# Scores and maxima of two heads in 64-row tiles: a pooled attention with a second stage of matmuls

## The chip, the cores and the metric

The kernel runs on one core of a Trainium2 chip. A core has five engines that run side by side and wait for each other through semaphores: TensorE (PE in the profile; PEld is its weight load), VectorE (DVE), ScalarE (ACT), GpSimd (POOL) and SyncE (SP, which issues the DMAs here). TensorE writes to PSUM, eight banks of 512 fp32 values on each of 128 partitions; DVE and ACT read from there. The metric is the device time of one execution in microseconds.

## The reference

Eight batches, eight heads, 1152 positions, 64 values per head. Neighbouring queries are averaged first, so that 576 queries meet 1152 keys:

```
q_pool = q.reshape(B, H, S // 2, 2, D).mean(axis=3)
scores = matmul(q_pool, k.T) / sqrt(D)
scores = scores - max(scores, axis=-1)
attn   = exp(scores);  attn = attn / (sum(attn, axis=-1) + 1e-9)
x      = matmul(attn, v)          # then heads side by side: 4608 tokens x 512
h      = x @ w_in                 # 512 -> 2048
out    = (h - tanh(h)) @ w_out    # 2048 -> 512
```

All arrays are fp32, and the results are compared as such. The row maximum is needed exactly enough that the exponentials do not overflow or lose precision.

## The kernel before

**Two stages.** The first (attention) goes over 32 pairs of heads: a batch `b` and two neighbouring heads, whose 64 values each fill the 128 partitions. The second goes over ten chunks of up to 512 tokens with the hidden layer in 16 tiles of 128 (`hidden`, L522, and `second`, L547).

**hi and lo.** TensorE's quick format (fp32r) keeps fewer bits than fp32, so an operand is split into `hi` (rounded, by ACT) and `lo` (what is left, by DVE), and a product is the sum hi x hi + hi x lo + lo x hi.

**A pair's life before its scores.** `load` fetches q and k; `query_sums` (L203) adds neighbouring queries; `hi_part` and `lo_part` split 576 queries and 1152 keys. `max_queries` (L219) copies hi's queries by DMA into a block-diagonal array `bd` of 9 x 128 columns: the first head's 576 queries on partitions 0 to 63, the second's after them on 64 to 127. `operands` (L225) builds by ten DMAs the arrays `t1` (128 rows: lo and hi of keys above hi and lo of queries) and `t2` (66 rows: hi, and two rows that bring in the maximum). `max_part` (L241) multiplies `bd` tiles with hi's keys, 27 matmuls of 384 columns, two to a PSUM tile `ps_m`, and DVE reduces each tile to its maximum. `max_rows` (L251) combines them, splits them in hi and lo, turns them by a transpose, and sends them through `m_dram` to the last two rows of `t2`.

**A pair's scores.** `score_unit` (L281) makes 128 keys x 288 queries of one head in one bank `ps_s` by two matmuls (128 rows and 66 rows), and ACT takes the exponential. Six units (two heads, three key tiles) are a group; a pair has two halves of the queries with three groups each. `z_part` adds up a group's exponentials on POOL. `pv` (L302) multiplies them with v, two heads side by side in the columns of the array; v and the exponentials are plain fp32, so each such matmul leaves two records. `z_sums` sums over partitions, four column tiles side by side.

**Order.** All engines of the first stage follow an order that is written out by hand: `U = 36` units make a pair, and `add(u, f)` puts a piece of work at unit `u`; `first` holds what a unit does before its scores. The numbers in L438 to L469 place each pair's preparation ahead of it, some 100 units for the loads, 60 to 27 for the maxima. `w_block` (L371) also lies in these units: it prepares the two weight matrices in 32 blocks with a chain of DVE, POOL and ACT steps and stores them split to DRAM.

**PSUM.** Two tiles of two banks `ps_m`, three banks `ps_s`, one `ps_o`: eight.

**Into the second stage.** Near the end (L422 to L435) the first chunk's x and six tiles of weights are fetched; the weights go where the operands `t1` and `t2` of even pairs were. The other weights follow at L514 to L520. The second stage's own PSUM tiles take the same eight banks.

Of the kernel before, what the change touches and what calls it, by code (L numbers as in the profile page):

```python
# [43 lines left out]
def kernel(  # L44
# [51 lines left out]
    def load_x(tiles, sp, mul, hi, t0, n):  # L96
# [5 lines left out]
        def fetch(hp):  # L102
            x = xt.tile([P, 512], F32, name="x_f")
            r = xt.tile([P, 512], F32, name="x_r")
            t[hp] = x, r
# [20 lines left out]

    xp = [ctx.enter_context(tc.tile_pool(name="xp0", bufs=2))]
# [4 lines left out]
    op0 = ctx.enter_context(tc.tile_pool(name="op0", bufs=1))  # L132
# [8 lines left out]
    with ExitStack() as actx:  # L141

        wp = actx.enter_context(tc.tile_pool(name="wp", bufs=1))
# [20 lines left out]
        tt = [[o.tile([P, 2, KQ], F32R, name=f"t{j}_{i}") for j in (1, 2)] for i, o in enumerate((op0, op))]  # L164
        t1, t2 = [t[0] for t in tt], [t[1][0:66] for t in tt]


        bd = [op.tile([P, 9 * P], F32R, name=f"bd{i}") for i in range(2)]
        for i in range(2):
            nc.gpsimd.memset(bd[i].bitcast(F32), 0.0)  # L170
            nc.gpsimd.memset(t2[i][64:66, :, SQ:].bitcast(F32), 1.0)

        def raw_copy(dst, src):
            sp.dma_start(dst.bitcast(F32), src.bitcast(F32))


        at, first = {}, {}
# [10 lines left out]
        def load(pi):  # L188
# [3 lines left out]
            w.t2 = t2[w.i]  # L192
# [10 lines left out]
        def query_sums(pi, eng):  # L203

            w = pairs[pi]
            eng.tensor_tensor(w.kq[:, 0:SQ], w.q_n[:, 0], w.q_n[:, 1], op=ALU.add)
            w.mx = sm.tile([P, 9, 3], F32, name="mx")
            w.hi = x_tile(0)[:, 0:KQ]
            w.lo = ld.tile([P, KQ], F32R, name="kq_l")
# [15 lines left out]
        def operands(pi):  # L225

            w = pairs[pi]
            for h in range(2):
                r = slice(h * 64, h * 64 + 64)
                x1, x2 = t1[w.i][:, h], t2[w.i][:, h]  # L230
                raw_copy(x1[0:64, SQ:], w.lo[r, SQ:])
                raw_copy(x1[64:P, 0:SQ], w.lo[r, 0:SQ])
                raw_copy(x1[64:P, SQ:], w.hi[r, SQ:])
                raw_copy(x1[0:64, 0:SQ], w.hi[r, 0:SQ])
                raw_copy(x2[0:64], w.hi[r])

        spots = [((j, j + 5), (c,)) for c in range(3) for j in range(4)] + [((4,), (0, 1)), ((4,), (2,))]

        def max_part(u, pi, ts, cs):  # L241

            w = pairs[pi]
            ps = ps_m.tile([P, 2, 512], F32, name="ps_m")
            both = [(t, c) for t in ts for c in cs]
            for i, (t, c) in enumerate(both):
                pe.matmul(ps[:, i, 0:CH], bd[w.i][:, t * P:(t + 1) * P], w.hi[:, SQ + c * CH:SQ + (c + 1) * CH], start=True, stop=True)
            mx = w.mx[:, ts[0]:ts[-1] + 1:5, cs[0]] if len(ts) == 2 else w.mx[:, 4, cs[0]:cs[-1] + 1]
            add(u + 1, lambda: dve.tensor_reduce(mx, ps[:, 0:len(both), 0:CH], axis=AX.X, op=ALU.max), at=first)

        def max_rows(u, pi, steps):  # L251
# [11 lines left out]
            def turn():  # L263
                ps = w.ps_t = ps_m.tile([P, 2, 512], F32R, name="ps_m")[0:20, 0, 0:P]
# [8 lines left out]
            def back():  # L273

                sp.dma_start(w.t2[64:66, :, 0:SQ].bitcast(F32), md.rearrange("s (h n) -> s h n", h=2)[:, :, 0:SQ])
# [5 lines left out]
        def score_unit(w, half, h, kt, p):  # L281
# [3 lines left out]
            ps = ps_s.tile([P, 512], F32, name="ps_s")  # L285
            x1, x2 = t1[w.i][:, h], t2[w.i][:, h]
# [35 lines left out]
        def z_sums(u, w, hf):  # L322

            ps = ps_s.tile([P, 512], F32, name="ps_s")
# [13 lines left out]
        def z_out(u, w, hf, ps):  # L338

            act.activation(w.z_s[:, hf.n * HQ:(hf.n + 1) * HQ], ps[:, 0:HQ], AF.Copy)  # L340
            if hf.n == 1:
# [4 lines left out]
                if w.hp == NP - 1:  # L346
                    add(u + 6, lambda: tot.append((w.b, sums(w.b))))
                    if w.b < B - 1:
                        add(u + 22, lambda: reciprocals(dve, *tot[0]))
                        add(u + 25, lambda: spread(sp, *tot.pop(0)))  # L350
# [20 lines left out]
        def w_block(u, kind, r, c):  # L371
# [44 lines left out]
        for i, blk in enumerate(blocks):  # L416
            u = U // 2 + 34 * i
# [11 lines left out]
        spare = [t.rearrange("p h n -> p (h n)")[:, i:i + 1024] for t in tt[0] for i in range(0, 3072, 1024)]  # L429
        wi, wo = [], []  # L430
        for i, (t, w_dram) in enumerate(((wi, wi_dram), (wi, wi_dram), (wi, wi_dram), (wo, wo_dram), (wi, wi_dram), (wo, wo_dram))):
            f = len(t)
            t.append(spare[i].rearrange("p (s c m) -> p s c m", s=2, c=NP) if t is wi else
                     spare[i].rearrange("p (s m) -> p s m", s=2))
            add(end - 17 + i, lambda x=t[f], y=w_dram[f]: sp.dma_start(x.bitcast(F32), y))  # L435


        for pi in range(n_pair):  # L438
            u = pi * U
            units = dict(load=-98, query_sums=-86, hi_q=-82, hi_k=-80, max_queries=-76, lo_q=-74, lo_k=-72, operands=-35, load_v=-30)  # L440
            row, steps = -26, (5, 8, 14)
            parts = [-60 + i * 33 // 14 for i in range(14)]
            step = 2
            if pi == 0:
                units.update(load=-70, query_sums=-60, hi_q=-59, hi_k=-58, max_queries=-57, lo_q=-56, lo_k=-55, operands=-54,
                             load_v=-50)
                row, steps, step = -32, (2, 4, 5), 0
                parts = [-46 + i for i in range(14)]
            if pi == 1:
                v0 = -U  # L450
                units.update(load=v0 - 69, query_sums=v0 - 31, hi_q=v0 - 30, hi_k=v0 - 29, max_queries=v0 - 28, lo_q=v0 - 27,
                             lo_k=v0 - 26, operands=v0 - 25)
                parts = [v0 + 2 + i * 20 // 14 for i in range(14)]
                row, steps, step = v0 + 23, (2, 4, 8), 0
            if pi == 2:
                units.update(query_sums=-80, hi_q=-76, hi_k=-74, max_queries=-70, lo_q=-66, lo_k=-64)
                parts = [-49 + i * 23 // 14 for i in range(14)]
            add(u + units["load"], load, pi)
            add(u + units["query_sums"], query_sums, pi, dve if pi < 2 else pool)
# [171 lines left out]
```

## Time and profile before

| what | value |
|---|---|
| three runs, us | 1828.22, 1828.22, 1825.83 (median 1828.22) |
| the profiled execution, us | 1825.99 |
| its span, us | 1824.2 |
| mean granted TensorE clock | 0.994 |
| first score matmul, last one, us from the start | 26.1, 989.4 |
| HBM read, written, MB | 109.64, 36.42 |
| DMA in all, MB | 242.29 |

A row of the timeline has the start, the time from the first start to the last end, the engine, the line, the operation, out<-in with shapes, how many instructions it merges, and in brackets the idle time before it with what ended that. Nearly all of the first stage stands under L37, the helper that records every instruction; there the names of tiles tell the instructions apart (`ps_m` maxima, `ps_s` scores and z sums, `ps_o<-p_f,v` PV, `ps_h` hidden sums of the second stage). `t` is any of `t1`, `t2`, and `x` is hi.

### The profile page before, as it was taken

Reading aid. Unit: us, or ns where it says so; the run is one execution under the profiler, and the core shown is the slowest. Engines: PE = TensorE matmul, PEld = TensorE weight load, DVE = VectorE, ACT = ScalarE, POOL = GpSimd, SP = SyncE. Lnnn points to the kernel's source line nnn. Section 1 sums busy time; section 2 is a strip of 40 time slices with the busy share of each in tenths; the row PEclk is TensorE's granted clock in tenths of the full one; section 3 lists DMA queues with packets and bytes.
Section 4 is the critical chain, followed back from the end, with each engine's and each line's share of the span. In section 5 each row is a group of like instructions: output and inputs, shape, how many; then the busy total and the mean of one; then the engine's idle time right before and its main releaser. Section 6 shows DMA issues by size and latency. Waiting matters only on the chain. (4 is left out here: it accounts for less than half of the span.)

```text
span 1824.2 us, 28257 instructions
## 1 busy us (share of the span) xinstructions
PE 1741.4 (95%) x9920; PEld 1306.6 (72%) x9920; DVE 1403.8 (77%) x1823; ACT 1084.0 (59%) x2473; POOL 1050.4 (58%) x756
## 2 busy tenths in 40 slices
PE   4999999999999989999998999999999999999998
PEld 3666666766676666666665777878787888788887
DVE  5776767677767777776741899988998899888897
ACT  2555555656565555555554655666666666666676
POOL 2666778777787767777864274353534444433433
PEclk9999999999999999999999999999999999999999
DMA  8767787878878676878763821020101010100000
GB/s 211 201 175 219 180 227 196 221 196 219 228 207 232 168 213 181 212 212 227 196 169 131 313 58 64 6 65 6 64 9 61 13 57 18 44 14 34 27 15 21
DMA packets 104141, 242.29 MB, mean 133 GB/s; under 512 B 18112, under 2 KB 43328, under 8 KB 104000
## 3 DMA queue, kind: packets, MB, share of 16 engines
q1 hardware_dynamic: 104000, 240.49, 47.7%
q8 instruction: 78, 1.28, 0.3%
q14 instruction: 63, 0.52, 0.1%
HBM read 109.64 MB, written 36.42 MB: 80 GB/s over the span
## 5 line engine op out<-in xcount | busy, mean ns | idle before, releaser
L37 DVE TENSOR_REDUCE mx<-ps_m 128x2 f32<-128x768 f32 x448 | 405.5, 924 | 258.2 <-PE ps_m L37 257.9
L37 ACT ACTIVATE p_f<-ps_s 128x288 f32<-128x288 f32 x1152 | 418.0, 411 | 193.6 <-PE ps_s L37 169.7
L37 PE MATMUL ps_s<-t 128*128 128x288 f32 (+1 forms) x2304 | 447.6, 313 | 15.1 <-ACT p_f L37 9.1
L544 POOL TENSOR_TENSOR g_lo<-g_s,g_hi 128x512 fp32r<-128x512 f32 (+1 forms) x160 | 209.2, 1308 | 414.3 <-ACT g_hi L543 360.0
L37 PEld LDWEIGHTS ps_s<-t 128*128 128x128 f32 (+1 forms) x2304 | 357.2, 191 | 120.0 <-issue 90.2
L37 POOL TENSOR_TENSOR z<-p_f 128x576 f32<-128x576 f32 x192 | 289.7, 1509 | 159.5 <-PE ps_s L37 112.0
L526 PE MATMUL ps_h<-x,wi 128*128 128x512 f32 (+1 forms) x1440 | 325.0, 370 | 1.4 <-DVE g_s L541 1.4
L37 PE MATMUL ps_o<-p_f,v 128*64 128x288 f32 x2304 | 325.7, 419 | 0.0
L37 POOL TENSOR_TENSOR z<-z,p_f 128x576 f32<-128x576 f32 x192 | 290.4, 1512 | 17.9 <-ACT p_f L37 3.2
L526 PEld LDWEIGHTS ps_h<-x,wi 128*128 128x128 f32 x1440 | 254.9, 188 | 53.4 <-ACT g_u L532 1.8
L551 PE MATMUL ps_o<-wo,g_hi 128*128 128x512 f32 x1008 | 275.7, 392 | 4.2 <-ACT g_hi L543 3.8
L37 PE MATMUL ps_m<-x,bd 128*128 128x384 f32 x864 | 237.7, 355 | 32.0 <-DVE mx L37 17.5
L37 PEld LDWEIGHTS ps_o<-p_f,v 128*64 128x64 f32 x2304 | 149.8, 138 | 114.8 <-issue 29.8
L551 PEld LDWEIGHTS ps_o<-wo,g_hi 128*128 128x128 f32 x1008 | 186.8, 188 | 46.3 <-ACT g_hi L543 7.4
L543 ACT ACTIVATE g_hi<-g_s 128x512 fp32r<-128x512 f32 (+1 forms) x160 | 94.3, 590 | 153.8 <-DVE g_s L542 151.5
L37 PEld LDWEIGHTS ps_m<-x,bd 128*128 128x128 f32 x864 | 143.5, 196 | 49.6 <-DVE mx L37 27.9
L539 DVE SCALAR_TENSOR_TENSOR g_w<-g_w,g_u 128x512 f32<-128x512 f32 (+1 forms) x160 | 172.6, 1079 | 0.0
L551 PE MATMUL ps_o<-wo,g_lo 128*128 128x512 f32 x504 | 160.1, 393 | 5.6 <-POOL g_lo L544 5.4
L532 ACT ACTIVATE g_u<-ps_h 128x512 f32<-128x512 f32 (+1 forms) x160 | 87.5, 547 | 119.5 <-PE ps_h L526 119.0
L542 DVE COPY_PREDICATED g_s<-g_m,g_t 128x512 f32<-128x512 int32 (+1 forms) x160 | 133.3, 833 | 14.7 <-DVE g_s L541 0.5
L540 DVE SCALAR_TENSOR_TENSOR g_w<-g_s,g_w 128x512 f32<-128x512 f32 (+1 forms) x160 | 129.3, 808 | 18.8 <-ACT g_s L534 2.2
L541 DVE SCALAR_TENSOR_TENSOR g_s<-g_s,g_w 128x512 f32<-128x512 f32 (+1 forms) x160 | 126.5, 790 | 17.0 <-ACT g_t L533 0.5
(60 smaller groups left out, 1887.8 us busy)
## 6 DMA issues: line engine op xcount, KB each, us to landing
t<-x SPq DMA_DIRECT2D x64, 432.0 KB
q_n<-in_q_dram SPq DMA_DIRECT2D x32, 576.0 KB
kq<-in_k_dram SPq DMA_DIRECT2D x32, 576.0 KB
t<-kq_l SPq DMA_DIRECT2D x64, 288.0 KB
t<-x SPq DMA_DIRECT2D x64, 288.0 KB
v<-in_v_dram SPq DMA_DIRECT2D x32, 576.0 KB
bd<-x SPq DMA_DIRECT2D x64, 144.0 KB
t<-kq_l SPq DMA_DIRECT2D x64, 144.0 KB
```

The lines of the kernel that those rows point to most:

```text
L37: ins = self.tc.keep_in_program_order(f(*args, **kwargs))
L526: nc.tensor.matmul(h, wi[fc][:, w, c], x[:, c, 0:n], start=(j == 0), stop=(j == len(mm) - 1))
L532: nc.scalar.activation(u, h, AF.Square)
L539: nc.vector.scalar_tensor_tensor(w, w, PL, u, op0=ALU.mult, op1=ALU.mult)
L540: nc.vector.scalar_tensor_tensor(w, s2, P2, w, op0=ALU.add, op1=ALU.mult)
L541: nc.vector.scalar_tensor_tensor(s1, s1, P1, w, op0=ALU.add, op1=ALU.mult)
L542: last = nc.vector.copy_predicated(s1, m.bitcast(I32), th).ins
L543: nc.scalar.activation(g_h, s1, AF.Copy)
L544: nc.gpsimd.tensor_tensor(g_l, s1, g_h.bitcast(F32), op=ALU.subtract)
L551: nc.tensor.matmul(po[j], g[:, ts], wo[fc][:, w], start=(fc == 0 and i == 0), stop=(fc == NF - 1 and i == 2))
```

## The change

- `hi` and `lo` get a pool of their own with three buffers each and are used in place. `bd`, `t1`, `t2` and the DMAs that filled them go. What is left of `bd` is one tile of 128 columns for the queries where the two heads meet; ACT copies its two corners (`middle`). The maximum's two rows per head go to `mb`, rows 0, 1 and 64, 65, the rest zero, and `ones_k` has ones in these rows.
- Scores: for one key tile and both heads, four matmuls per head of 64 rows each (hi x hi, hi x lo, lo x hi, ones x maximum), the heads in turn, each into its own bank of a two-bank tile. One exponential takes both banks, 576 columns.
- Maxima: 24 of the 27 become matmuls of 64 rows, two heads in turn; three (the meeting tile) stay at 128 rows.
- PSUM: three two-bank tiles `ps_s` that scores and maxima share, one bank `ps_z` (z sums, meeting tile, transpose), one `ps_o`.
- Times: a new list `early` runs ahead of a unit's scores. Each group has a maximum tile ahead of its first score tile and one after its last, and three groups of a pair have a meeting tile ahead of PV. The row maxima's steps, the loads, the splits and the weight blocks' steps get new units; weight blocks start every 36 units instead of every 34.
- x of the first chunk is fetched from 58 units before the end instead of 18, into the buffers of q and k; eight tiles of weights instead of six from 100 units before the end, into memory of their own.

```diff
-    op0 = ctx.enter_context(tc.tile_pool(name="op0", bufs=1))
+    wt0 = ctx.enter_context(tc.tile_pool(name="wt0", bufs=1))
...
+        hl = actx.enter_context(tc.tile_pool(name="hl", bufs=3))
...
-        ps_m = actx.enter_context(tc.tile_pool(name="ps_m", bufs=2, space=PSUM))
         ps_s = actx.enter_context(tc.tile_pool(name="ps_s", bufs=3, space=PSUM))
+        ps_z = actx.enter_context(tc.tile_pool(name="ps_z", bufs=1, space=PSUM))
...
-        bd = [op.tile([P, 9 * P], F32R, name=f"bd{i}") for i in range(2)]
+        mb = [op.tile([P, SQ], F32R, name=f"mb{i}") for i in range(2)]
+        ones_k = op.tile([P, P], F32R, name="ones_k")
+        bd = [op.tile([P, P], F32R, name=f"bd{i}") for i in range(2)]
...
-        def max_queries(pi):
-            w = pairs[pi]
-            for h in range(2):
-                r = slice(h * 64, h * 64 + 64)
-                raw_copy(bd[w.i][r, h * SQ:(h + 1) * SQ], w.hi[r, 0:SQ])
+        def middle(pi):
+            w = pairs[pi]
+            act.activation(bd[w.i][0:64, 0:64], w.hi[0:64, 512:SQ].bitcast(F32), AF.Copy)
+            act.activation(bd[w.i][64:P, 64:P], w.hi[64:P, 0:64].bitcast(F32), AF.Copy)
...
+            cs = slice(SQ + c * CH, SQ + (c + 1) * CH)
+            if t < 4:
+                ps = ps_s.tile([P, 2, 512], F32, name="ps_s")
+                for h in range(2):
+                    r = slice(64 * h, 64 * h + 64)
+                    pe.matmul(ps[:, h, 0:CH], w.hi[r, 64 * h + t * P:64 * h + (t + 1) * P], w.hi[r, cs], start=True, stop=True)
+                add(u + 1, lambda: dve.tensor_reduce(w.mx[:, t:t + 6:5, c], ps[:, :, 0:CH], axis=AX.X, op=ALU.max), at=first)
+            else:
+                ps = ps_z.tile([P, 512], F32, name="ps_z")
+                pe.matmul(ps[:, 0:CH], bd[w.i], w.hi[:, cs], start=True, stop=True)
...
-            ps = ps_s.tile([P, 512], F32, name="ps_s")
-            x1, x2 = t1[w.i][:, h], t2[w.i][:, h]
-            pe.matmul(ps[:, 0:HQ], x1[:, ks], x1[:, qs], start=True, stop=False)
-            pe.matmul(ps[:, 0:HQ], x2[:, ks], x2[:, qs], start=False, stop=True)
-            act.activation(p, ps[:, 0:HQ], AF.Exp, scale=1.0 / 16)
+            ps = ps_s.tile([P, 2, 512], F32, name="ps_s")
+            for i, (x, y) in enumerate(((w.hi[:, ks], w.hi[:, qs]), (w.hi[:, ks], w.lo[:, qs]), (w.lo[:, ks], w.hi[:, qs]),
+                                        (ones_k, w.mb[:, qs]))):
+                for h in range(2):
+                    r = slice(64 * h, 64 * h + 64)
+                    pe.matmul(ps[:, h, 0:HQ], x[r], y[r], start=(i == 0), stop=(i == 3))
+            act.activation(p, ps[:, :, 0:HQ], AF.Exp, scale=1.0 / 16)
...
-        add(end - 19, lambda: x0.extend(load_x(lambda: (x_tile(0), x_tile(0)), sp, dve,
+        add(end - 60, lambda: x0.extend(load_x(lambda: (x_tile(0), x_tile(0)), x0_raw, sp, dve,
...
-            for i, x in enumerate((0, 5, 6, 7)):
-                add(end - 18 + 7 * j + x, lambda i=i, j=j: x0[2][j][i]())
+            for i, x in enumerate((0, 12, 14, 17)):
+                add(end - 58 + 6 * j + x, lambda i=i, j=j: x0[2][j][i]())
...
-            add(end - 17 + i, lambda x=t[f], y=w_dram[f]: sp.dma_start(x.bitcast(F32), y))
+            t.append(wt0.tile([P, 2, NP, P] if t is wi else [P, 2, DM], F32R, name=f"w0{i}"))
+            add(end - 100 + 8 * i, lambda x=t[f], y=(wi_dram if t is wi else wo_dram)[f]: sp.dma_start(x.bitcast(F32), y))
...
-            row, steps = -26, (5, 8, 14)
-            parts = [-60 + i * 33 // 14 for i in range(14)]
+            units = dict(load=-92, query_sums=-80, hi_q=-70, hi_k=-68, hi_k2=-66, lo_q=-64, lo_k=-52, lo_k2=-46, load_v=-40)
+            row, steps = -23, (4, 6, 12)
+            spots = [x for g in range(6) for x in ((at, -60 + G * g + 5), (early, -60 + G * g + 6))]
+            mids = [-49, -37, -31]
```

More of the change, by code (lines that the diff above doesn't have):

```diff
@@ L159 @@
         G = 6
-        tt = [[o.tile([P, 2, KQ], F32R, name=f"t{j}_{i}") for j in (1, 2)] for i, o in enumerate((op0, op))]
-        t1, t2 = [t[0] for t in tt], [t[1][0:66] for t in tt]
-        bd = [op.tile([P, 9 * P], F32R, name=f"bd{i}") for i in range(2)]
[L169 to L177, printed above, removed]
+        mb = [op.tile([P, SQ], F32R, name=f"mb{i}") for i in range(2)]
+        ones_k = op.tile([P, P], F32R, name="ones_k")
+        bd = [op.tile([P, P], F32R, name=f"bd{i}") for i in range(2)]
+        for x in (*mb, *bd, ones_k):
+            nc.gpsimd.memset(x.bitcast(F32), 0.0)
+        for h in range(2):
+            nc.gpsimd.memset(ones_k[64 * h:64 * h + 2].bitcast(F32), 1.0)
+        at, first, early = {}, {}, {}
         end = n_pair * U
@@ L207, in query_sums @@
             w.mx = sm.tile([P, 9, 3], F32, name="mx")
-            w.hi = x_tile(0)[:, 0:KQ]
-            w.lo = ld.tile([P, KQ], F32R, name="kq_l")
+            w.hi = hl.tile([P, KQ], F32R, name="hi")
+            w.lo = hl.tile([P, KQ], F32R, name="lo")
         def hi_part(pi, c0, c1):
@@ L227, in operands, with max_part @@
+        def max_part(u, pi, t, c):
             w = pairs[pi]
-            for h in range(2):
-                r = slice(h * 64, h * 64 + 64)
-                x1, x2 = t1[w.i][:, h], t2[w.i][:, h]
[L231 to L239, printed above, removed]
@@ L241, in max_part @@
-        def max_part(u, pi, ts, cs):
-            w = pairs[pi]
[L244 to L249, printed above, removed]
+            cs = slice(SQ + c * CH, SQ + (c + 1) * CH)
@@ new lines, in max_part @@
+            if t < 4:
[7 more added lines that the diff above has]
+                pe.matmul(ps[:, 0:CH], bd[w.i], w.hi[:, cs], start=True, stop=True)
+                add(u + 1, lambda: dve.tensor_reduce(w.mx[:, 4, c:c + 1], ps[:, 0:CH], axis=AX.X, op=ALU.max), at=first)
@@ L263, in turn @@
             def turn():
-                ps = w.ps_t = ps_m.tile([P, 2, 512], F32R, name="ps_m")[0:20, 0, 0:P]
+                ps = w.ps_t = ps_z.tile([P, 512], F32R, name="ps_z")[0:20, 0:P]
                 pe.transpose(ps, m2.rearrange("p s h t -> p (s h t)"), ident_r)
@@ L273, in back @@
             def back():
-                sp.dma_start(w.t2[64:66, :, 0:SQ].bitcast(F32), md.rearrange("s (h n) -> s h n", h=2)[:, :, 0:SQ])
+                for h in range(2):
+                    sp.dma_start(w.mb[64 * h:64 * h + 2].bitcast(F32), md[:, h * (5 * P + 64):h * (5 * P + 64) + SQ])
             add(u + steps[0], turn)
@@ L322, in z_sums @@
         def z_sums(u, w, hf):
-            ps = ps_s.tile([P, 512], F32, name="ps_s")
+            ps = ps_z.tile([P, 512], F32, name="ps_z")
             for g in range(3):
@@ L444 @@
+            mids = [-49, -37, -31]
             if pi == 0:
[L445 to L454, printed above, removed]
@@ L455 @@
-            if pi == 2:
-                units.update(query_sums=-80, hi_q=-76, hi_k=-74, max_queries=-70, lo_q=-66, lo_k=-64)
-                parts = [-49 + i * 23 // 14 for i in range(14)]
+                units.update(load=-60, query_sums=-52, hi_q=-51, hi_k=-50, hi_k2=-49, lo_q=-22, lo_k=-21, lo_k2=-20)
+                spots = [(at, -48 + 2 * i) for i in range(12)]
+                mids = [-43, -35, -27]
+                row, steps = -24, (2, 3, 4)
+            if pi < 3:
+                v0 = -U * pi
+                if pi == 1:
+                    units.update(load=v0 - 58, query_sums=v0 - 25, hi_q=v0 - 20, hi_k=v0 - 19, hi_k2=v0 - 18, lo_q=-28, lo_k=-16, lo_k2=-10)
+                    mids = [v0 + 5, v0 + 11, v0 + 17]
+                    row, steps = v0 + 25, (2, 3, 6)
+                if pi == 2:
+                    mids = [v0 + 29, v0 + 35, v0 + 41]
+                if pi > 0:
+                    spots = [x for g in range(4) for x in ((early, v0 + 24 * (pi - 1) + G * g), (at, v0 + 24 * (pi - 1) + G * g + 2),
+                                                           (at, v0 + 24 * (pi - 1) + G * g + 5))]
@@ L462 @@
                 add(u + units[what + "_k"], f, pi, SQ, 2 * SQ)
-                add(u + units[what + "_k"] + step, f, pi, 2 * SQ, KQ)
-            add(u + units["max_queries"], max_queries, pi)
-            for x, part in zip(parts, spots):
-                add(u + x, max_part, u + x, pi, *part)
-            add(u + units["operands"], operands, pi)
+                add(u + units[what + "_k2"], f, pi, 2 * SQ, KQ)
+            add(u + units["hi_k2"], middle, pi)
+            for i, (when, x) in enumerate(spots):
+                add(u + x, max_part, u + x, pi, *divmod(i, 3), at=when)
+            for c, x in enumerate(mids):
+                add(u + x, max_part, u + x, pi, 4, c)
             add(u + units["load_v"], load_v, pi)
@@ L477 @@
             run(u, first)
+            run(u, early)
             run(u)
@@ L481 @@
             run(u, first)
-            if u < end:
+            run(u, early)
+            if u < end and u % 2 == 0:
                 pi, r = divmod(u, U)
@@ L503 @@
                 pv(u, groups[n])
-        assert not any(at.values())
+        assert not any(x for t in (at, first, early) for x in t.values())
     wt = ctx.enter_context(tc.tile_pool(name="wt", bufs=1))
```

64 lines of the change are left out of this document (30 added, 34 removed).

## The prediction

> **What bounds the kernel now.** I read the page first (engine shares), then busy time by stretches, then TensorE's timeline in a steady pair, then groups and waits.
>
> ```profile
> span 1824.2 us, 28257 instructions
> PE 1741.4 (95%) x9920; PEld 1306.6 (72%) x9920; DVE 1403.8 (77%) x1823; ACT 1084.0 (59%) x2473; POOL 1050.4 (58%) x756
> ```
>
> ```profile
> 60.00:940.00 880.00, 849.28 (x5783) 592.80 (x5783) 633.89 (x789) 503.86 (x1356) 653.45 (x444) 0.99 0.77 205
> 940.00:980.00 40.00, 39.26 (x265) 25.18 (x264) 5.68 (x12) 23.47 (x68) 29.18 (x21) 1.00 0.47 143
> 980.00:1001.00 21.00, 14.29 (x87) 8.52 (x88) 3.98 (x6) 5.63 (x14) 5.63 (x4) 0.85 0.44 140
> ```
>
> The columns are PE, weight load, DVE, ACT, POOL, granted clock, DMA share. In the attention stage (60 to 940) TensorE is busy 849 of 880 us, DVE 634, POOL 653, ACT 504: TensorE sets the pace. But a matmul's record covers its latency too, so what counts is start to start. The timeline of TensorE gives those prices:
>
> ```profile
> 500.70 1.68 PE L37 MATMUL ps_o<-p_f,v 128*64 128x288 f32 x12
> 502.31 0.81 PE L37 MATMUL ps_s<-t 128*128 128x288 f32 x4
> 502.95 0.51 PE L37 MATMUL ps_m<-x,bd 128*128 128x384 f32 x2
> 503.30 0.70 PE L37 MATMUL ps_s<-t 128*128 128x288 f32 x4
> 503.84 0.51 PE L37 MATMUL ps_m<-x,bd 128*128 128x384 f32 x2
> ...
> 504.72 0.51 PE L37 MATMUL ps_m<-x,bd 128*128 128x384 f32 x2
> 505.17 1.68 PE L37 MATMUL ps_o<-p_f,v 128*64 128x288 f32 x12
> ...
> 510.89 1.16 PE L37 MATMUL ps_s<-z,ones 128*32 128x288 f32 x12
> 511.98 0.53 PE L37 MATMUL ps_s<-t 128*128 128x288 f32 x2
> ```
>
> Two max matmuls take 503.30 - 502.95 = 0.35 us, so 0.175 each; four score matmuls 503.84 - 503.30 = 0.54, so 0.135 each. The PV block takes 502.31 - 500.70 = 1.61, the z sums 511.98 - 510.89 = 1.09. Where the shape of the tiles changes there is a toll on either side: the first four scores after PV take 0.64 (502.31 to 502.95) instead of 0.54, the last two max matmuls before PV 0.45 (504.72 to 505.17) instead of 0.35: 0.10 each way.
>
> A pair has six groups (12 scores, one PV block), 27 max matmuls, two z sums and a transpose of about 0.1: 6 x (1.62 + 1.61 + 0.20) + 27 x 0.175 + 2 x 1.09 + 0.1 = 27.6 us. The transposes, one per pair, show what a pair really takes:
>
> ```profile
> 58.65 0.23 PE L37 MATMUL ps_m<-ident_r,m 128*20 128x128 f32 x1
> ...
> 946.14 0.22 PE L37 MATMUL ps_m<-ident_r,m 128*20 128x128 f32 x1
> ```
>
> These are pairs 1 and 31: 887.5 / 30 = 29.58 us. So 2.0 us per pair are stalls. The view of the maxima names most of them (weight load and matmul waits, partly the same time):
>
> ```profile
> PEld ps_m L37: 34.2, 41
> PE ps_m L37: 22.6, 28
> ```
>
> **The change, part by part.**
>
> *Scores.* Two matmuls of 128 and 66 rows per head become four of 64 rows per head, the two heads alternating on the two halves of the rows and on two PSUM banks. If the halves run side by side, four pairs cost what four matmuls cost: 4 x 0.135, no change. No row here shows row halves. The nearest rows are the column tiles, whose weights load and whose matmuls run side by side:
>
> ```profile
> 500.70 0.20 PEld L37 LDWEIGHTS ps_o<-p_f,v 128*64 128x64 f32 x4 [0.16 <-issue]
> ...
> 510.88 0.16 PEld L37 LDWEIGHTS ps_s<-z,ones 128*32 128x32 f32 x8 [0.44 <-issue]
> ```
>
> Eight loads of 32 columns lie within 0.16 us, four of 64 within 0.20. And the z block packs its twelve records into 1.16 us, where PV's take 1.68 with two side by side. Bounds for a pair: 0.135 (full overlap) and 0.27 (none). I take 0.135, the end that the column tiles are nearest to.
>
> The Trainium skill, "TensorE: Matmul & The Clock Gate", section "Measured speedup vs the span model", gives 3.07 times for four row tiles; taken as a rate, its 4/3.07 = 1.30 makes a pair 0.176, an estimate from that page; no run here shows it yet, and it is the third rival's case.
>
> *Maxima.* 24 of the 27 matmuls become 12 pairs; three (the tile that holds both heads) stay whole. Saved: 12 x 0.175 = 2.1 us a pair. Each whole one sits just ahead of a PV block, with another shape on both sides: one change more, 0.20, so 3 x 0.20 = 0.6 back (bounds 0 and 1.0: twice the toll at most if both sides pay).
>
> *Shared PSUM.* The real price. Before, maxima had two buffers and scores three; now both rotate through three two-bank buffers, five tiles a group: M1, S1, S2, S3, M2. S3 takes M1's buffer, so it waits for M1's reduction.
>
> ```profile
> L37 ACT ACTIVATE p_f<-ps_s 128x288 f32<-128x288 f32 x1059 | 385.0, 412 | 176.2 <-PE ps_s L37 153.5 <-PE ps_m L37 0.4
> L37 DVE TENSOR_REDUCE mx<-ps_m 128x2 f32<-128x768 f32 x388 | 363.5, 953 | 235.3 <-PE ps_m L37 235.0
> ...
> L37 DVE TENSOR_TENSOR kq_l<-kq,x 128x576 fp32r<-128x576 f32 x87 | 97.2, 1117 | 0.0
> ...
> L37 DVE CAST m<-nm 128x10 fp32r<-128x10 f32 x29 | 23.5, 809 | 1.0
> ```
>
> ```profile
> 503.50 2.73 DVE L37 TENSOR_REDUCE mx<-ps_m 128x2 f32<-128x768 f32 x3 [1.02 <-PE ps_m L37]
> ```
>
> Count from the end of a PV block. M1 pays 0.10 and streams 0.175; its record outlasts that by 0.16 (0.51 for two = 0.175 + 0.335): data at 0.435. The reduction starts 0.04 later (the two max matmuls of 502.95 end at 503.46, the reduction starts at 503.50) and takes 0.953: done at 1.43. With 0.05 for the signal and 0.10 for a weight load that could not run ahead (both estimates, the second from the toll above), S3 streams from 1.58. TensorE is ready at 0.275 + 8 x 0.135 = 1.36. So each group stalls 0.22. Then S3 0.54 and M2 0.175: 2.30; toll and PV 1.71: a group takes 4.01 us. M2 needs S1's exponentials: S1's data stand at 0.98, one 576-wide exponential costs at most two of the old, 0.82, so 1.84, before 2.12. M1 and S1 of the next group need S2's and S3's, with a PV block between: hidden.
>
> *The transposes.* Row maxima are now combined one slot after the last M1 and turned four slots later, right after M2. The cast alone takes 0.81 after the reduction's 1.43, and with three smaller instructions I estimate the result at 2.8, where TensorE arrives at 2.30: 0.5 a pair, PV queued behind it.
>
> *A pair:* 6 x 4.01 + 3 x 0.375 + 2 x 1.09 + 0.1 + 0.5 = 27.97 us. Other stalls (DVE or ACT late for another reason) I put at 0.7, a third of today's 2.0, as the reductions that caused most of those now have slots of their own; bounds 0 and 1.7. So 28.6 against 29.58: 30 x -0.95 = **-29 us**.
>
> *Costed at nothing.* The twelve copies per pair that built bd and the operands go (384 DMAs): no engine's wait in the steady stage is on them, and the DMA share of 0.77 falls. ACT gets two copies of a 64-wide corner, DVE a 15th reduction; ACT was busy 504 of 880 and DVE 634. Uncovered, the copies would cost at most 32 x 2 x 0.41 = 26 us. The weight blocks' steps now fall into fixed slots after M1's reduction. Loads of q, k, v move a few slots; on SP's queue they have twelve fewer instructions in front.
>
> *The last pair.* Without maxima twelve scores take 954.42 - 952.26 = 2.16, where 1.62 + 0.20 would do: the exponentials hold it, six of 0.41 in a row.
>
> ```profile
> 952.26 2.23 PE L37 MATMUL ps_s<-t 128*128 128x288 f32 x12
> 954.42 1.68 PE L37 MATMUL ps_o<-p_f,v 128*64 128x288 f32 x12
> ```
>
> Three wide ones fit better: 0.34 x about 9 groups = **-3 us**.
>
> *The head.*
>
> ```profile
> 5.48 1.89 ACT L37 ACTIVATE x<-kq 128x576 fp32r<-128x576 f32 x3 [3.47 <-DVE kq L37]
> ```
>
> ```profile
> 10.09 1.72 PE L37 MATMUL ps_m<-x,bd 128*128 128x384 f32 x4 [10.09 <-DMA bd<-x]
> ...
> 32.59 1.54 PE L37 MATMUL ps_s<-t 66*128 66x288 f32 x5 [5.89 <-DMA t<-m_dram]
> ```
>
> The first maxima wait for bd until 10.09, though hi is whole at 7.37. Without bd they start there: **-3 us**. The chain through m_dram stays.
>
> *The start of the second stage.*
>
> ```profile
> 987.56 1.75 PE L526 MATMUL ps_h<-x,t 128*128 128x512 f32 x4 [1.98 <-ACT x L37]
> ...
> 1000.59 10.55 PE L526 MATMUL ps_h<-x,t 128*128 128x512 f32 x36 [4.73 <-ACT x L37]
> ```
>
> TensorE waits 1.98 + 4.73 us for x there, and the granted clock of 0.85 costs about one more. The fetches move forty slots ahead, onto an SP queue with only stores beside them; DVE, which divides x, was busy 5.7 of 40 us there. But six of the eight PSUM banks now belong to the scores until their last exponential, so the first hidden sums cannot slip in between the last scores any more; the last PV and z blocks cover that. I take **-7 us** (bounds 0 and -9).
>
> **Sum**, against the profiled execution: 1824.2 - 29 - 3 - 3 - 7 = 1782 span, and with the 1.8 that lie around it (1825.99 less 1824.2) 1784 us. The median shown, 1828.22, is 2 us above that execution, which is about what a measurement of this kernel cannot tell from no change (0.2%, 3.7 us).
>
> **The rivals.**
>
> 1. *Late reductions (slower).* All now hangs on M1's reduction starting at once. Any DVE instruction in front of it delays S3, PV and the whole group one for one; the candidates are lo parts (1.117 us), weight steps and the reduction of M2. For it: DVE is busy 72% and the view of the maxima shows TensorE waiting for it today, with two spare buffers. Against: by the slots, DVE has only M2's reduction and a little more during 1.7 us of PV. Break-even is 44 / 192 groups = 0.23 us of delay on average. At 0.35: +67, **1851**.
>
> 2. *No overlap.* If the halves run one after the other, a pair of scores costs 0.27: 72 x 0.135 + 12 x 0.175, less the stall at S3 (1.3), +10.5 us a pair: about **2120**. This is also the case in which the change does not do what it says. Against it stand the column tiles.
>
> 3. *Partial overlap (slower).* Let a pair cost k matmuls. A group up to PV is 0.10 + k x (0.35 + 1.62), once the stall at S3 is filled by it; break-even, 2.30 + 0.23 = 2.53, is at k = 1.23. At k = 1.3, under a third of the way to no overlap: 2.66, +0.36 x 192 = +69, **1853**. For it: two result streams into the same PSUM partitions, which no row here shows. Against: column tiles cost nothing extra, whether two or four lie side by side.
>
> 4. *The second stage gains nothing*, since PSUM keeps it waiting: **1791**, within the forecast's own range.
>
> **How the numbers follow.** Forecast (with the fourth) 68%, own range 1762 to 1815: other stalls of 0 and 1.7 a pair move it by -21 and +30. Below that, with the transposes hidden too, down to 1748: 5%. Late reductions 9%, partial overlap 13% (k anywhere above 1.15: 1820 to 1880), no overlap 5%. Range 1752 to 1856: outside lie no overlap, the upper third of rivals 1 and 3, and the lowest few per cent, about 18%. Faster by over 0.2%: 68 + 5 and the mild part of rival 3, 0.74. Within: 0.04. Slower: 0.22.
>
> **What will show it.** Right: two 64-row matmuls starting within about 0.01 us, the next two 0.135 later; transposes 28.6 us apart; TensorE waiting about 0.2 us for a reduction ahead of the third score tile of each group, and about 0.5 at a transpose; no hidden-sum wait for x. Wrong: pairs 0.17 or more apart (rivals 2, 3); waits at the third score tile far over 0.2 with DVE busy before the reduction (rival 1); or no such wait and pairs near 27 us apart, which would say that the shared buffers cost less than I count.

## The result, and the profile after

The changed kernel takes **1806.57 us** (median; 1805.21 to 1809.5) where the kernel before, timed beside it, takes 1828.22 (1825.83 to 1829.24): a ratio of 0.9886, 95% interval 0.9868 to 0.9903. It is faster by 21.7 us. The forecast was 44 us, so the sign and the range held and half of the gain did not come. The page of the profiled execution (1805.21 us) begins:

```profile
span 1803.4 us, 31496 instructions
PE 1705.4 (95%) x12224; PEld 1238.7 (69%) x12224; DVE 1454.6 (81%) x1854; ACT 1049.1 (58%) x1961; POOL 1038.6 (58%) x760
```

The span fell by 20.8 us. To see in which stage, take the transposes on TensorE's timeline, the same marks that the prediction used. The first three rows are pairs 0, 1 and 31 after, in brackets what TensorE stood idle for just ahead of each:

```profile
20.26 0.28 PE L37 MATMUL ps_z<-ident_r,m 128*20 128x128 f32 x1 [2.69 <-DVE m L37]
49.39 0.23 PE L37 MATMUL ps_z<-ident_r,m 128*20 128x128 f32 x1 [1.21 <-DVE m L37]
...
935.79 0.22 PE L37 MATMUL ps_z<-ident_r,m 128*20 128x128 f32 x1 [1.90 <-DVE m L37]
```

And the same view before, pair 0 (pairs 1 and 31, at 58.65 and 946.14, stand in the prediction):

```profile
25.88 0.27 PE L37 MATMUL ps_m<-ident_r,m 128*20 128x128 f32 x1 [1.75 <-DVE m L37]
```

| stretch | before | after | difference | forecast |
|---|---|---|---|---|
| start to pair 0's transpose | 25.88 | 20.26 | -5.6 | -3 |
| pair 0 to pair 1 | 32.77 | 29.13 | -3.6 | 0 |
| 30 steady pairs, 1 to 31 | 887.5 | 886.4 | **-1.1** | **-29** |
| last transpose to the end | 878.1 | 867.6 | -10.4 | -3 - 7 |
| span | 1824.2 | 1803.4 | -20.8 | -42 |

Head and tail gave what was counted on or more. The steady stage, where nearly all of the work was saved, gave next to nothing: a pair takes 886.4 / 30 = 29.55 us against 29.58 before. (The first of these 30 intervals holds only 26 of a pair's 36 units, in both kernels: 23.97 us before, 23.89 after. So a full pair is 29.78 and 29.74 us, and the prediction's 2.0 us of stalls in a pair before are 2.2; the difference between the kernels stays.) But TensorE has less to do in it. The busy time of the stretch 60 to 920 (columns as in the prediction: PE, weight load, DVE, ACT, POOL, clock, DMA share):

```profile
60.00:920.00 860.00, 806.33 (x7761) 521.38 (x7759) 658.63 (x798) 464.41 (x869) 626.52 (x433) 0.99 0.34 109
```

The busy share of PE went from 849.28 / 880 = 0.965 to 806.33 / 860 = 0.938. So the matmuls were saved and a wait stands where they were. The view of the waits in the same stretch (in all, times, longest) names it:

```profile
PEld ps_z L37 <- DVE m L37: 53.5, 28, 2.2
PEld ps_s L37 <- DVE mx L37: 46.3, 170, 1.4
PE ps_z L37 <- DVE m L37: 45.8, 28, 1.9
```

At 28 transposes TensorE waits 45.8 us for m, the combined row maxima: 1.64 us each, where the forecast had 0.5. Here is what happens ahead of one, on all engines:

```profile
518.07 0.96 DVE L37 TENSOR_REDUCE mx<-ps_s 128x2 f32<-128x768 f32 x1 [2.12 <-PE ps_s L37]
...
518.82 1.42 POOL L37 TENSOR_TENSOR z<-z,p_f 128x576 f32<-128x576 f32 x1
519.06 0.24 DVE L37 TENSOR_REDUCE nm<-mx 128x5 f32<-128x15 f32 x2
...
519.08 0.40 PE L37 MATMUL ps_s<-hi 64*128 64x288 f32 x2
...
519.32 0.30 PE L37 MATMUL ps_s<-lo,hi 64*128 64x288 f32 x2
519.34 0.93 DVE L37 CAST m<-nm 128x10 fp32r<-128x10 f32 x1
519.45 0.30 PE L37 MATMUL ps_s<-hi,lo 64*128 64x288 f32 x2
519.71 0.35 PE L37 MATMUL ps_s<-hi 64*128 64x384 f32 x2
520.20 1.39 POOL L37 TENSOR_TENSOR z<-p_f 128x576 f32<-128x576 f32 x1
520.30 1.32 DVE L37 TENSOR_TENSOR m<-nm,m 128x10 fp32r<-128x10 f32 x1
521.54 0.95 DVE L37 TENSOR_REDUCE mx<-ps_s 128x2 f32<-128x768 f32 x1
521.67 0.23 PE L37 MATMUL ps_z<-ident_r,m 128*20 128x128 f32 x1 [1.62 <-DVE m L37]
521.83 1.68 PE L37 MATMUL ps_o<-p_f,v 128*64 128x288 f32 x12
```

Two instructions over ten columns last 0.93 and 1.32 us. Now lay POOL's rows beside them. The cast ends at 520.27, POOL's first addition at 520.24. The subtraction ends at 521.62, POOL's second addition at 521.59. Both end 0.03 us after an instruction of POOL with which they have nothing to do. TensorE has sent M2 at 519.71 and then stands until 521.67, with the PV block queued behind the transpose. The view of the tile m shows the durations (min/median/max, ns), first after, then before:

```profile
L37 DVE CAST m<-nm x32: 173/931/1221, 19.8 to 933.4; 128x10 fp32r<-128x10 f32 x32
L37 DVE TENSOR_TENSOR m<-nm,m x32: 169/1316/1328, 20.0 to 934.3; 128x10 fp32r<-128x10 f32 x32
```

```profile
L37 DVE CAST m<-nm x32: 173/902/1242, 25.4 to 941.6; 128x10 fp32r<-128x10 f32 x32
L37 DVE TENSOR_TENSOR m<-nm,m x32: 169/170/1397, 25.6 to 941.8; 128x10 fp32r<-128x10 f32 x32
```

Alone, each takes 0.17 us. Before, the cast already waited most of the time, but the subtraction mostly slipped through, at 0.17. After, it meets POOL's next addition too.

### The profile page after: what moved, and what is told of

Same layout as the page of the kernel before. It is cut to its first block, busy times and chain, and to the rows that moved or that the text cites. A ratio compares the mean times of both kernels' runs of the same rounds, so it can differ in the third digit from the quotient of the medians.

```text
span 1803.4 us, 31496 instructions
## 1 busy us (share of the span) xinstructions
PE 1705.4 (95%) x12224; PEld 1238.7 (69%) x12224; DVE 1454.6 (81%) x1854; ACT 1049.1 (58%) x1961; POOL 1038.6 (58%) x760
## 4 chain that ended last, share of the span: by engine, by line
PE 71%; DVE 17%; DMA 4%; ACT 4%; POOL 3%; issue 2%; SPq 1%; DVEq 0%; POOLq 0%; ACTq 0%
PE ps_s L37 20%; PE ps_o L37 16%; PE ps_h L525 14%; PE ps_o L550 14%; PE ps_z L37 6%; DVE m L37 4%; DVE mx L37 3%; DVE g_s L541 2%; DVE g_w L539 1%; DVE g_s L540 1%; DMA x_f<-x_dram 1%; DMA x_r<-r_dram 1%; DVE g_w L538 1%; POOL g_lo L543 1%; DVE lo L37 1%
## 5 line engine op out<-in xcount | busy, mean ns | idle before, releaser
L37 DVE TENSOR_REDUCE mx<-ps_s 128x2 f32<-128x768 f32 x384 | 364.9, 953 | 211.0 <-PE ps_s L37 209.6
L37 ACT ACTIVATE p_f<-ps_s 128x576 f32<-128x576 f32 x576 | 352.6, 649 | 249.9 <-PE ps_s L37 227.8
L37 PE MATMUL ps_s<-hi 64*128 64x288 f32 (+1 forms) x1920 | 316.8, 358 | 19.0 <-ACT hi L37 8.6
L525 PE MATMUL ps_h<-x,wi 128*128 128x512 f32 (+1 forms) x1320 | 295.8, 369 | 0.0
L37 PEld LDWEIGHTS ps_s<-hi 64*128 64x128 f32 x1920 | 170.5, 189 | 152.4 <-issue 73.3
L525 PEld LDWEIGHTS ps_h<-x,wi 128*128 128x128 f32 x1320 | 233.6, 188 | 47.4
L37 PE MATMUL ps_s<-mb,ones_k 64*128 64x288 f32 x1152 | 171.9, 293 | 3.3 <-DMA mb<-m_dram 3.3
L37 PE MATMUL ps_s<-lo,hi 64*128 64x288 f32 x1152 | 172.9, 295 | 0.0
L37 PE MATMUL ps_s<-hi,lo 64*128 64x288 f32 x1152 | 172.3, 294 | 0.0
L536 DVE SCALAR_TENSOR_TENSOR g_w<-g_u,ps_h 128x512 f32<-128x512 f32 (+1 forms) x160 | 100.3, 627 | 61.1 <-ACT g_t L532 39.4
```

What stands on the lines that cost most here:

```text
L37: ins = self.tc.keep_in_program_order(f(*args, **kwargs))
L525: nc.tensor.matmul(h, wi[fc][:, w, c], x[:, c, 0:n], start=(j == 0), stop=(j == len(mm) - 1))
L536: nc.vector.scalar_tensor_tensor(w, u, -P0, h, op0=ALU.add, op1=ALU.mult)
```

## The experiments

**The theory:** the cast and the subtraction cannot run beside an addition on POOL, and TensorE now waits for them at the transpose. **The rivals:** the gain went to late reductions and the shared PSUM tiles; or the row halves overlap only in part; or the matmuls' order matters. In the table's "pair" column stand the 30 steady intervals between transposes, divided by 30 (the short first one lowers it by up to 0.2 us).

| kernel | median us | ratio to the kernel before, 95% | pair us |
|---|---|---|---|
| the changed kernel | 1806.57 | 0.9886, 0.9868 to 0.9903 | 29.55 |
| transpose one slot later | 1752.17 | 0.9596, 0.9580 to 0.9612 | 27.82 |
| POOL's additions split | 1742.56 | 0.9542, 0.9527 to 0.9556 | 27.54 |
| reductions for cast and subtraction | 1743.03 | 0.9544, 0.9529 to 0.9559 | 27.60 |
| both of these | 1739.03 | 0.9524, 0.9509 to 0.9539 | 27.44 |
| both of these in the kernel before | 1807.03 | 0.9889, 0.9867 to 0.9910 | 28.89 |
| reductions, and M1's over half the keys | 1693.95 | 0.9278, 0.9263 to 0.9293 | 26.00 |
| reductions, and maxima on one row half | 1803.56 | 0.9878, 0.9861 to 0.9894 | 29.51 |
| head by head | 1804.65 (one run) | | 29.60 |
| late fetch of x and weights | 1817.03 | 0.9950, 0.9931 to 0.9970 | 29.58 |

**The transpose one slot later.** The same instructions; the transpose goes behind M1 and S1 of the next group, and the two DMAs after it move one slot too.

```diff
-            row, steps = -23, (4, 6, 12)
+            row, steps = -23, (5, 7, 13)
```

> The transpose is moved by one unit, from ahead of PV to behind the next group's first maximum and score tiles (some 2.5 us later for TensorE). Theory L (the wait of 1.6 to 1.9 us at each of the 31 transposes is what ate the gain, because the cast and the subtraction ahead of it each wait for a POOL addition): the wait vanishes, the tile shapes change once more (0.3 us), a pair falls from 29.55 to 28.0 us and the time to about 1760. Rival P (the wait is not what sets the pair: the shared PSUM buffers or ACT would hold TensorE as long): pairs stay within 0.3 us of 29.5, time 1798 to 1808.

Measured: 1752.17 us, 54 less than the changed kernel. TensorE's timeline, pairs 1 and 31:

```profile
48.92 0.23 PE L37 MATMUL ps_z<-ident_r,m 128*20 128x128 f32 x1 [1.21 <-DVE m L37]
...
883.39 0.23 PE L37 MATMUL ps_z<-ident_r,m 128*20 128x128 f32 x1
```

The steady transposes no longer wait, and a pair is 1.73 us shorter, which is the wait (1.64) and a little more. This shows that the wait at the transpose was the lost gain. It doesn't show why m was late: the median of the subtraction is still 1.325 us in this kernel.

**POOL's additions split.** The two additions that sum the exponentials for z become four over one head each; DVE is left alone.

```diff
-            pool.tensor_tensor(z, grp.p[:, :, 0], grp.p[:, :, 1], op=ALU.add)
-            pool.tensor_tensor(z, z, grp.p[:, :, 2], op=ALU.add)
+            for h in range(2):
+                pool.tensor_tensor(z[:, h], grp.p[:, h, 0], grp.p[:, h, 1], op=ALU.add)
+                pool.tensor_tensor(z[:, h], z[:, h], grp.p[:, h, 2], op=ALU.add)
```

> Each of POOL's two additions over both heads becomes two over one head each: the same sums, half the length (about 0.75 us). Theory L (a small DVE instruction waits until POOL's addition in flight ends): cast and subtraction wait for half as long, 0.93 + 1.32 us become about 0.5 + 0.7, the wait at the transpose falls from 1.7 to about 0.7, time about 1775. Rival S (these DVE instructions are slow by themselves there, or DVE shares bandwidth with POOL in proportion): their durations stay within 0.1 us, time 1800 to 1810.

Measured: 1742.56 us. The view of the tile m:

```profile
L37 DVE CAST m<-nm x32: 172/485/494, 19.8 to 874.2; 128x10 fp32r<-128x10 f32 x32
L37 DVE TENSOR_TENSOR m<-nm,m x32: 169/169/712, 20.0 to 874.7; 128x10 fp32r<-128x10 f32 x32
```

Only POOL was edited, and DVE's instructions became shorter: the cast from a median of 0.931 to 0.485 us, the subtraction from 1.316 to 0.169. So POOL held them. The expectation had the subtraction at 0.7 us and some wait left; it mostly slips in between two of the shorter additions instead, and TensorE stands idle ahead of only 3 of the 32 transposes.

**Reductions in their place.** POOL is left alone; cast and subtraction become three reductions over one or two elements, which give the same numbers (maximum of one; its negative; the sum of two).

```diff
-            nm = sm.tile([P, 2, 5], F32, name="nm")
+            nm = sm.tile([P, 2, 5, 2], F32, name="nm")
...
-            dve.tensor_copy(m2[:, 0], nm)
-            dve.tensor_tensor(m2[:, 1], nm, m2[:, 0].bitcast(F32), op=ALU.subtract)
+                dve.tensor_reduce(m2[:, 0], nm[:, :, :, 0:1], axis=AX.X, op=ALU.max)
+                dve.tensor_reduce(nm[:, :, :, 1], m2[:, 0].bitcast(F32).rearrange("p h (t o) -> p h t o", o=1), axis=AX.X, op=ALU.max, negate=True)
+                dve.tensor_reduce(m2[:, 1], nm, axis=AX.X, op=ALU.add)
```

> The cast and the subtraction of the 128x10 row maxima are written as three small reductions (over one, one and two elements), a form that at this place takes 0.12 to 0.16 us beside POOL's additions in the trace. Theory L: the row maxima stand about 0.75 us after M1's reduction instead of 2.6, no wait at the transpose, no drop of the granted clock behind it, pairs at 27.7 us, time about 1750. Rival S (small instructions wait in that place whatever their form): three of 0.9 us or more, time above 1806. Rival P: wait gone, time 1798 to 1808.

Measured: 1743.03 us. The view of m:

```profile
L37 DVE TENSOR_REDUCE m<-nm x64: 164/170/177, 19.8 to 877.0; 128x10 fp32r<-128x10 f32 x32, 128x10 fp32r<-128x20 f32 x32
L37 DVE TENSOR_REDUCE nm<-m x32: 164/165/167, 20.0 to 876.8; 128x10 f32<-128x10 f32 x32
```

The longest of 96 takes 0.177 us, with POOL as busy as before. Three instructions that are never held beat two that are. These two experiments edit different engines and meet at the same time; together they show the cause. The Trainium skill, "SBUF — State Buffer", section "Who interferes with whom", has the rule: a VectorE instruction with two inputs in SBUF, or a cast in a two-port mode, and a GpSimd instruction share a pair of ports as an exclusive lock, so that whichever comes second waits for the whole of the other, while a reduction on trn2 never contends. The traces here agree in each of the three: 1.316 us against 0.169 for the subtraction, 0.931 against 0.173 for the cast, 0.177 at most for a reduction. That this cast runs in such a mode, no row here shows.

**Both edits together**, on the changed kernel:

> e2_split_z and e3_reduce together. e2_split_z has pairs of 27.67 us without exception, e3_reduce 27.50 with every fourth near 28.4, where a four-fold longer chain (reciprocals of the sums) meets POOL's full-length additions. Both together: 27.5 throughout, 7 us under either, about 1736. If the fourth pair's 0.9 us has another cause: 1742.

Measured: 1739.03 us (1737.61 to 1741.12), the best kernel here that computes everything. Pairs 1 and 31:

```profile
48.85 0.23 PE L37 MATMUL ps_z<-ident_r,m 128*20 128x128 f32 x1 [0.31 <-DVE m L37]
...
872.09 0.22 PE L37 MATMUL ps_z<-ident_r,m 128*20 128x128 f32 x1 [0.18 <-DVE m L37]
```

(872.09 - 48.85) / 30 = 27.44 us a pair. After the short first interval all are 27.54 to 27.60 us: every fourth pair, about 28.4 in the kernel with reductions alone, no longer stands out. But most pairs are 0.07 us longer than the 27.50 there, and the two edits together gain about 4 us over either, not the 7 expected.

**Both edits in the kernel before.** Is it the change that made the lock expensive, or did both kernels pay?

> The kernel before with the same two edits as e8_both (row maxima by three small reductions, POOL's additions in halves) and nothing of the change. If POOL's additions cost the kernel before little (its transposes wait 0.2 to 0.3 us): 1815 to 1826, and the change without this wait is worth about 80 us. If the same waits made up its 2.0 us of stalls a pair: 1770 or less, and the two edits, not the 64-row tiles, are what e8_both gains.

Measured: 1807.03 us against 1827.46 beside it. The edits gain 20 us there and 67 us in the changed kernel. The view of the maxima in this kernel, which answers the two rows shown in the prediction, says where:

```profile
PEld ps_m L37: 17.0, 34
PE ps_m L37: 7.5, 19
```

TensorE's waits for the maxima fall from 34.2 and 22.6 us to 17.0 and 7.5. So half and more of the waits that the prediction took for late reductions went with the two edits, and a pair goes from 29.58 to 28.89. The result lies between the two cases expected: the lock cost the kernel before something, but it was not most of its stalls. With both edits on either side the change is worth 1807.0 - 1739.0 = **68 us**.

**M1's reduction over half the keys** (on the kernel with reductions). It leaves half the keys of these tiles out of the row maximum; the matmuls stay.

```diff
-                add(u + 1, lambda: dve.tensor_reduce(w.mx[:, t:t + 6:5, c], ps[:, :, 0:CH], ...
+                add(u + 1, lambda: dve.tensor_reduce(w.mx[:, t:t + 6:5, c], ps[:, :, 0:n], ...
...
-                add(u + x, max_part, u + x, pi, *divmod(i, 3), at=when)
+                add(u + x, max_part, u + x, pi, *divmod(i, 3), CH // 2 if when is early else CH, at=when)
```

> On top of e3_reduce: the reduction of each group's first maximum tile (M1) takes in half of its columns; what is left out is half of the keys of that tile in the row maximum, which only scales the exponentials. The reduction falls from 0.95 to about 0.55 us. Theory of the prediction (S3 waits about 0.22 us per group for M1's reduction because they share a PSUM buffer): the wait goes in all but the first and last pair, 6 x 0.22 = 1.3 us a pair, pairs from 27.5 to 26.2, time from 1743 to about 1703. Rival (an exponential or the next reduction holds TensorE as long when this wait is gone): pairs stay above 27.2, time 1733 to 1743.

Measured: 1693.95 us, a pair 26.00 instead of 27.60. DVE's groups from 60 to 800, short and whole reductions apart:

```profile
L37 DVE TENSOR_REDUCE mx<-ps_s 128x2 f32<-128x384 f32 x168 | 93.9, 559 | 149.6 <-PE ps_s L37 149.4
L37 DVE TENSOR_REDUCE mx<-ps_s 128x2 f32<-128x768 f32 x172 | 163.7, 952 | 42.8 <-PE ps_s L37 42.8
```

M1's reduction is 0.39 us shorter, and TensorE's weight loads wait 5.4 us in all for the maxima instead of 53.8. Most pairs go from 27.50 to 26.03: 1.47 / 6 = 0.245 us a group, the wait of S3 that the prediction put at 0.22.

**The maxima of both heads on one row half** (on the kernel with reductions). It leaves out the second head's own maximum; the count and size of the matmuls stay, but they can't lie side by side.

```diff
                 for h in range(2):
                     r = slice(64 * h, 64 * h + 64)
+                    r = slice(0, 64)
```

> On top of e3_reduce: both matmuls of a maximum tile read the first head's row half, so they cannot run side by side; left out is the second head's own maximum (the first head's takes its place, which only scales the exponentials). If overlap is what saves the 0.175 us per tile: each of 12 tiles a pair costs 0.175 more, M1's reduction starts as much later, +2.1 us a pair, 31 pairs: +65, about 1808. If the waits for the reductions hide it: M2's share alone or less, below 1775.

Measured: 1803.56 us. A pair of max matmuls on TensorE's timeline:

```profile
503.71 0.50 PE L37 MATMUL ps_s<-hi 64*128 64x384 f32 x2
```

In the changed kernel the pair at 519.71 takes 0.35. Most pairs of heads go from 27.50 to 29.52 us: +2.02, where the prediction has 12 x 0.175 = 2.1 for what side by side saves.

**Head by head.** The four score matmuls of head 0, then the four of head 1, on the changed kernel.

```diff
-            for i, (x, y) in enumerate(...):
-                for h in range(2):
+            for h in range(2):
+                for i, (x, y) in enumerate(...):
```

> The same eight score matmuls per tile, but four of the first head and then four of the second, instead of the heads in turn. If matmuls of 64 rows cost nothing extra only because neighbours in the queue lie on different row halves: a score tile takes 7 to 8 x 0.13 instead of 4 x 0.13 us, +0.4 to 0.5 us x 576, less the 0.2 us stall at each third tile that this fills: about 2020 to 2070. If TensorE finds the overlap whatever the order: unchanged, 1800 to 1812.

Measured: 1804.65 us in one run, a pair 29.60: no different. That overlap needs the heads to alternate in the program was wrong. TensorE's timeline:

```profile
500.63 0.41 PE L37 MATMUL ps_s<-hi 64*128 64x288 f32 x2
500.87 0.31 PE L37 MATMUL ps_s<-lo,hi 64*128 64x288 f32 x2
```

A head has one matmul of each form in a tile, so the two in a row are one of each head, though the second head's stands four places later in the program. In what order the compiled program holds them is not in the trace.

**The late fetch.** x and the first weights are fetched where they were before the change; all else is the changed kernel.

```diff
-        add(end - 60, lambda: x0.extend(load_x(...
+        add(end - 19, lambda: x0.extend(load_x(...
-            for i, x in enumerate((0, 12, 14, 17)):
-                add(end - 58 + 6 * j + x, lambda i=i, j=j: x0[2][j][i]())
+            for i, x in enumerate((0, 5, 6, 7)):
+                add(end - 18 + 7 * j + x, lambda i=i, j=j: x0[2][j][i]())
-            add(end - 100 + 8 * i, lambda x=t[f], ...
+            add(end - 17 + i, lambda x=t[f], ...
```

> The changed kernel with the first x and the eight weight tiles fetched as late as before (18 and 17 units before the end), nothing else undone. If the earlier fetch is worth what was predicted: 7 us slower than the changed kernel, about 1814, with the wait of TensorE for x back at the start of the second stage. If the scores' PSUM banks or the last PV blocks hold the second stage anyway: within 2 us of 1806.6.

Measured: 1817.03 us, 10.5 more than the changed kernel by medians. The stretch from the last transpose to the end takes 1810.6 - 936.7 = 873.9 us in the profiled execution, against 867.6: 6.3 of it lie there. So the earlier fetch carries 6 to 10 of the 10.4 us that the tail gave. The path is not quite the one predicted: the waits of TensorE from 940 to 1100 in this kernel are

```profile
PE ps_o L37 <- ACT p_f L37: 3.5, 1, 3.5
...
PE ps_h L525 <- ACT x L37: 0.7, 1, 0.7
```

and the 6.7 us for x of before have not come back as a wait of the hidden sums. ACT's exponentials are late instead, and ACT's timeline says by which instruction:

```profile
976.64 0.63 ACT L37 ACTIVATE x<-q_n 128x512 fp32r<-128x512 f32 x1 [4.67 <-DVE q_n L37]
977.18 1.17 ACT L37 ACTIVATE p_f<-ps_s 128x576 f32<-128x576 f32 x2
```

ACT's copy of x stands ahead of the last two exponentials in its order. It waits 4.67 us for DVE's division, which in turn waits 6.14 us for the fetch of the reciprocals. So TensorE does wait for the late x, by way of ACT.

## Why the prediction was wrong about the size, and what of it held

**The step that failed is "The transposes".** It put the result of the combined maxima at 2.8 us after PV and TensorE at 2.30, a wait of 0.5. From M1's reduction's end to the transpose it had 2.8 - 1.43 = 1.37 us. Measured in the timeline above: 519.03 to 521.67, 2.64. With the instructions at their own 0.17 it would be 0.24 + 0.17 + 0.17 and small gaps, under 0.8. The fault was in the reading: the quoted 0.81 us for a cast of ten columns was taken as its length, when it is mostly a wait for POOL, and the subtraction's mean in the kernel before (0.445 us) hid the same wait behind the many times it got through. Worse, the step priced the instructions where they stood before, not where they would stand: a lock's price depends on what runs beside it.

The rest of that sum holds closely. Its pair without other stalls was 27.97 us. With the measured 2.64 the result stands at 1.43 + 2.64 = 4.07, 1.77 after TensorE's 2.30; with 1.77 instead of 0.5 the pair is 29.24. Fourteen of the 30 intervals are 29.18 to 29.25. And without any wait there, 27.97 - 0.5 = 27.47; the kernel with reductions takes 27.50 in most pairs, the one with both edits 27.57.

- **"Other stalls 0.7"** weren't there in such a pair, as these two equalities show. So two errors stood against each other: 1.27 too little at the transpose, about 0.4 too much here on the mean of the 30 intervals.
- **The mean, 29.55, above 29.21** has two sources. Six intervals, 30.5 to 30.8 us, are those in which the granted clock falls after the long wait; seven, every fourth pair, are 30.1 to 30.4. Together they are some 15 us longer than 13 of 29.21; the short first interval, 5.3 less, lies against that. For the first source, busy time by stretches, and TensorE's timeline in it:

```profile
219.00:226.00 7.00, 5.78 (x41) 3.45 (x41) 3.94 (x5) 1.62 (x5) 2.54 (x2) 0.76 0.43 154
```

```profile
220.22 0.23 PE L37 MATMUL ps_z<-ident_r,m 128*20 128x128 f32 x1 [1.63 <-DVE m L37]
220.38 3.15 PE L37 MATMUL ps_o<-p_f,v 128*64 128x288 f32 x12
```

  The PV block takes 3.15 us instead of 1.68. The other: in every fourth pair an instruction of DVE stands ahead of M2's reduction. It ends 0.05 us after an addition of POOL, at 292.44, so that POOL seems to hold it too. M2's reduction and, behind it, M1's of the next group come late, and S3 of that group waits 0.87 us. POOL, DVE, then TensorE:

```profile
290.50 1.94 POOL L37 TENSOR_TENSOR kq<-q_n 128x576 f32<-128x576 f32 x1
```

```profile
291.09 1.40 DVE L37 SCALAR_TENSOR_TENSOR rec<-rec 128x36 f32<-128x36 f32 x1
292.52 0.38 DVE L37 RECIPROCAL rec<-rec 128x36 f32<-128x36 f32 x1
292.82 0.90 DVE L37 TENSOR_REDUCE mx<-ps_s 128x2 f32<-128x768 f32 x1
```

```profile
295.48 0.40 PE L37 MATMUL ps_s<-hi 64*128 64x288 f32 x2 [0.87 <-DVE mx L37]
```

- **Scores, k = 1:** right. 519.32 and 519.45 are two pairs of row halves, 0.13 us apart, the price of one full matmul. Rivals 2 and 3 fall. The rate that the prediction worked out from the Trainium skill, "TensorE: Matmul & The Clock Gate", section "Measured speedup vs the span model", 0.176 a pair, isn't seen here.
- **Maxima, 2.1 a pair:** right, 2.02 by experiment. The three whole matmuls at 0.6 were not measured alone; the sums above leave no room for much else.
- **Shared PSUM, 0.22 a group:** right, 0.245 by experiment. The estimate of 0.05 for the signal held too: M1's reduction ends at 519.03, and S3 starts at 519.08.
- **Rival 1, late reductions:** only in every fourth pair, as above. It is nearest to what happened, DVE's work that comes late, but it had S3 wait, and what waited was the transpose.
- **Rival 4:** wrong; the second stage gained.
- **The head:** -5.6 instead of -3, and from pair 0 to pair 1 another -3.6 that was not counted. After:

```profile
6.92 1.58 PE L37 MATMUL ps_s<-hi 64*128 64x384 f32 x6 [6.92 <-ACT hi L37]
...
22.17 0.93 PE L37 MATMUL ps_s<-hi 64*128 64x384 f32 x4 [1.64 <-ACT hi L37]
...
26.84 0.76 PE L37 MATMUL ps_s<-mb,ones_k 64*128 64x288 f32 x2 [3.26 <-DMA mb<-m_dram]
```

  The maxima start at 6.92 instead of 10.09, the step's 3 us. They also take 10.65 us instead of 14.04, with the halves side by side from the start, and the transpose then waits 0.9 longer for m: together the 5.6. The chain through m_dram did stay: 26.84 - 20.26 = 6.6 us from the transpose to the first complete score, against 32.59 - 25.88 = 6.7. TensorE stands idle in it for 1.64 + 3.26 = 4.90 us instead of 5.89, since more score and max matmuls can run under it: 1.0 of the 3.6. The other 2.6 were not traced.
- **The tail:** -10.4 against -10. The 6.7 us that TensorE waited for x are gone, as told. But the earlier x costs something that was not counted: its copy now holds ACT, with the copy of PV's result behind it, and TensorE waits 2.55 us for that one. So that the size came out right is in part luck. ACT, then TensorE:

```profile
957.15 0.63 ACT L37 ACTIVATE x<-kq 128x512 fp32r<-128x512 f32 x1 [2.94 <-DVE kq L37]
957.69 0.39 ACT L37 ACTIVATE o_s<-ps_o 128x288 f32<-128x288 f32 x1
```

```profile
958.13 3.11 PE L37 MATMUL ps_o<-p_f,v 128*64 128x288 f32 x12 [2.55 <-ACT o_s L37]
```

## What to carry to other kernels

Read the minimum beside the median of an instruction: a ten-column instruction that takes 0.17 us at best and 0.9 at the median is probably waiting, and if it ends where another engine's instruction ends, suspect that one and test it by an edit of either side. Before moving such an instruction onto the path, ask what will run beside it in its new place, and write it in a form that isn't held or shorten what holds it. A forecast that adds up instruction times from rows can be right to 0.1 us in 28 and still miss by half, when one of the rows is a wait.

## What the hardware showed that was not expected

- A VectorE cast or subtraction of 128x10, 0.17 us alone, takes up to 1.22 and 1.33 us beside GpSimd in the changed kernel; reductions of the same size take 0.18 at most. The two edits that avoid or shorten this gain 67 us of 1806 in this kernel.
- Matmuls on different row halves don't keep the program's order: in the head-by-head kernel the second head's first matmul starts beside the first head's first, four places ahead of its turn. The Trainium skill, "TensorE: Matmul & The Clock Gate", section "The mechanism", calls matmuls strictly first in, first out in start and end; the trace here differs, and the unchanged pair time (29.60) goes with the trace. That the compiled program had them in another order is not excluded.
- A wait of 1.6 us of TensorE was followed in 6 of 28 cases by a lower granted clock: 0.76 on the mean of 219 to 226, with the PV block behind the wait at 3.15 us instead of 1.68.
